# Zero products in TensorE's waits, halved fp32 casts, and batch 1 masked by VectorE in a fused attention and FFN kernel

## The chip, the cores and the metric

The kernel runs on one core of one Trainium2 chip. A core has five engines which run their own instruction queues in order: TensorE (PE in the profile; its weight loads are PEld), VectorE (DVE), ScalarE (ACT), GpSimd (POOL) and SyncE (SP). They wait for one another by semaphores. Transfers are issued from the queues of POOL, SP and ACT. The metric is the device time of one execution in microseconds; the median of five runs is compared.

## The reference

Attention with 8 heads over 8 batches of 576 positions of 64, followed by a multiplicative FFN.

```python
scores = scale * np.matmul(q, k.transpose(0, 1, 3, 2))
rel = pos[:, None] - pos[None, :]
mask_plain = (rel >= 0) & (rel < 32)
mask_dil = (rel >= 0) & (rel < 128) & (rel % 4 == 0)
# heads 0-3 take mask_plain, heads 4-7 mask_dil; softmax over the masked scores
x = attn_out, as 4608 tokens of 512
out = ((x @ w1) * (x @ w2)) @ w3 @ w_out
```

w1 and w2 are 512 x 1024, w3 is 1024 x 1024, w_out 1024 x 512. All tensors are float32 in memory. The kernel multiplies in bf16.

## The kernel before

Attention is done in blocks of 96 queries against 128 keys. A batch has two head halves u (0 plain, 1 dilated) of six blocks each. The FFN is done in units of 288 tokens, two to a batch.

The kernel writes out every piece of work as a task with an engine, an estimated duration and a priority, and a planner (class Plan) lays the tasks out in time and gives each a PSUM bank. The order that results is the program order of each engine's queue. The planner's times have no other part in the run: at run time an engine simply waits, in its queue, for the semaphores of what it needs. The tables RANK, ON_DVE and FIRST_LOADS set priorities, which evacuations VectorE does instead of ScalarE, and the order of the weight loads.

The names of the tasks, with batch b, half u and step i (two steps in each u):

- T: VectorE turns q, k and v into columns (`turn`, in 32 x 32 squares); C casts the first q and k from float32 on ScalarE (`round_rows`). Only these two transfers, the u = 0 half of q and k of batch 0, come in float32 through SP; every other load is converted on the way by POOL's transfers. POOL's transfers have eight semaphores in turn, so the ninth waits in the queue until the first has landed.
- S: the scores of a group of blocks on TensorE (`Group.scores`), in four PSUM banks; E: their exponential on ScalarE (`exps`). The task is named after its first block: S0.3 is the last of the four groups of batch 0. Batches below BIASED have groups of three blocks, in which four products of the identity with a 288-column bias first put the mask into PSUM (L400). The others have groups of GRP = 5, which run on across batches, and VectorE multiplies the exponentials by a 0/1 mask, half a group at a time (M, L436). The masks are made by GpSimd out of the bias.
- VT and VK: for batches 0 and 1 v is transposed on TensorE (`v_back`) and written back by ScalarE, or by VectorE for names in ON_DVE (`v_keep`).
- V: probabilities times v for one step (`Step.values`); R and N: reciprocal and normalization on VectorE; X: back transpose on TensorE for batches 0 and 1, K: its copy to XT (`keep`). Later batches use a transposing transfer on SP.
- W3T, W3C, W3M, W3D: per block of 128 rows of w3, transpose on TensorE (eight products of 128 columns), copy to w3T on ScalarE, product with w_out (eight of 512 columns), copy to wf_sb. So w3 and w_out are merged into one matrix inside the kernel.
- A, B: up-projections of a unit by w1 and w2, four products of 288 columns each (L525), with CA (copy on ScalarE) and G (product on VectorE); Y: down-projection, eight products of 512 columns (L552).

The first A needs the copies K0.0, K0.1 and K0.2. The first two units are done for the lower half of the w1, w2 columns and then for the upper. Each S is tied to a certain A, so that it doesn't run too early (LEAD).

Of the kernel before, what the change touches and what calls it, by code (L numbers as in the profile page):

```python
# [10 lines left out]
P = 128  # L11
# [17 lines left out]
BIG = 30000.0  # L29
BIASED = 2  # L30
TURNED = 2
DIRECT_V = 2
ORDER = (2, 3, 0, 1)
RES = (0, 2, 1, 3)
RANK = dict(E=3, VK=1, K=1.5, N=0.4, T=0.4, VT=0.4, S=0.3, V=0.05, X=0.4)
WARM = 12
FIRST_LOADS = ("30", "w0", "w1", "w2", "q1", "31", "k1", "o0", "o1", "32", "33", "34", "v1", "35", "36", "37")
SHIFT = {}
ON_DVE = ("K0.0", "K0.1", "K0.2", "K1.1", "K1.2", "K1.3", "VK1.1.0", "W3D3", "W3D4", "W3D7")
GRP = 5  # L40
WHOLE = ("qn", "kn")
BUSY = 4500
LEAD = 1.2

# [12 lines left out]
class Plan:  # L57
# [6 lines left out]
    def __init__(self):  # L64
        self.tasks, self.now, self.dma = [], None, 0.0

    def add(self, name, eng, dur, deps, fn, prio, slot=0, lat=150, after=()):
# [3 lines left out]

    def run(self):
        users = {id(t): [] for t in self.tasks}
        takers = {id(t): [] for t in self.tasks}
# [39 lines left out]
        while len(order) < n:  # L114
            progress = True
            while progress:
                progress = False
                for e in engines:
                    if free[e] > now:
                        continue  # L120
                    for r, t in sorted(waiting[e], key=lambda x: x[1].prio):
                        if r > now:
                            continue
                        at = place(t) if t.slot else 0
                        if at is not None:
                            break
                    else:
                        continue
                    waiting[e].remove((r, t))
                    t.start = now  # L130
                    if e == "DMA":
                        free[e] = now + t.dur[0]
                        if t.dur[1]:
                            dma = max(dma, now + t.dur[0]) + t.dur[1]
                            t.end = dma + 1900
                        else:
                            t.end = free[e]
                    else:
                        t.end = free[e] = now + t.dur
                        if e == "SP" and t.name[0] == "X" and dma > now:  # L140
                            t.end = free[e] = now + t.dur + BUSY
                            dma += 1.5 * t.dur
                    if t.slot:
                        t.place = at
                        held[at : at + t.slot] = [t] * t.slot
                        if t.slot == 4:
                            kept = None
                    order.append(t)
                    for u in users[id(t)]:
                        left[id(u)] -= 1  # L150
                        if not left[id(u)]:
                            r = max(d.end + (0 if d.eng == u.eng else d.lat) for d in u.deps)
                            waiting[u.eng].append((r, u))
                    progress = True
# [6 lines left out]
            now = min(ahead)  # L161
        return sorted(order, key=lambda t: t.start), now


@with_exitstack
def kernel(
# [74 lines left out]

    def round_rows(nm, u):
        at = {"qn": 0, "kn": 18 * D, "vn": 36 * D}[nm]
        if (nm, 0) not in qk:
            qk[(nm, 0)] = qk_pool.tile([P, 2, 18 * D], BF16, tag=nm, name=nm)
        nc.scalar.copy(out=qk[(nm, 0)][:, u, :], in_=stage[:, at : at + 18 * D])  # L246

# [95 lines left out]
    def turn(b, u, nm, part):  # L343


        src = qk[(nm, b)][:, u, :].bitcast(U32)
        dst, pad = {"qn": (qts, 0), "kn": (kts, PADK), "vn": (vts, PADK)}[nm]
        d = dst[b % len(dst)].rearrange("p u w c -> p u (w c)").bitcast(U32)[:, u, :]
        if part is None:
            o = d[:, pad : pad + S].rearrange("p (j a) -> p a j", a=18)  # L350
            nc.vector.transpose(out=o, in_=src.rearrange("p (a i) -> p a i", a=18))  # L351
            return
# [270 lines left out]
    add = plan.add  # L623

    def warm_up():
        o = bank(512)
# [7 lines left out]
    def constants():  # L634
# [5 lines left out]
        for t in vps:  # L640
            nc.vector.memset(t[:, :, :, D : D + 1], 1.0)
            nc.vector.memset(t[0:32, :, 0, 0:D], 0.0)

    c1 = add("const", "DVE", 1200, [], first_constants, -99)
    c0 = add("const2", "DVE", 1400, [c1], constants, -98)
    add("warm", "PE", 1840 + 216 * WARM, [c1], warm_up, 0)

# [37 lines left out]
    for i, nm in enumerate(WHOLE):  # L685
        t = add(f"LF{nm}", "SP", 100, [], lambda nm=nm: load_whole(nm, rows_of[nm], 0), -9 + i,
                lat=4400 + 1350 * i)
        L[(nm, 0, 0)] = add(f"C{nm}", "ACT", 1120, [t], lambda nm=nm: round_rows(nm, 0), -9 + i,
                            lat=100)
    plan.dma = 1200 + 1350 * len(WHOLE)  # L690
# [24 lines left out]
    for ft in sorted(lw3):  # L715
        x = add(f"W3T{ft}", "PE", 510, [lw3[ft], idt], lambda f=ft: w3_back(f), 6, slot=1,
                after=w3m[-3:-2])
        y = add("W3C", "ACT", 1012, [x], lambda f=ft: w3_keep(f), -1, lat=100, after=w3m[-3:-2])
        if ft + 7 in lw3:
# [12 lines left out]
    def turns(b, u, nm, pr):  # L732

        if u == 0:
            parts = (None,) if nm != "qn" else (0, 1)
        else:
            parts = (2, 3, 4, 5) if b == 0 else (0, 1)
        old = last_v.get((b - 1, u)) if nm == "vn" else last_s.get((b - 2, u))
        cost = {None: 1245, 0: 750, 1: 630, 2: 430, 3: 370, 4: 430, 5: 370}
        ts = [  # L740
            add(f"T{nm}{b}.{u}.{part or 0}", "DVE", cost[part], [L[(nm, b, u)], c0],
                lambda part=part: turn(b, u, nm, part), pr + (1 if part in (4, 5) else 0), lat=80,
# [5 lines left out]

    vals, T = {}, {}
    for b in range(B):  # L750
# [4 lines left out]
        for u in range(2):  # L755
            tk = turns(b, u, "kn", 10 * b + RANK["T"])
            tq = turns(b, u, "qn", 10 * b + RANK["T"])
            for hf in range(2):
                T[(b, u, hf)] = tk[hf] + tq[hf]
        for u in range(2):  # L760
            if b >= DIRECT_V:
                break
            tv = turns(b, u, "vn", 10 * b + RANK["T"])
            for half in range(2):
                x = add(f"VT{b}.{u}.{half}", "PE", 420, tv[half] + [idt],
                        lambda b=b, u=u, h=half: v_back(b, u, h), b - 99 + RANK["VT"], slot=1)
                last_v[(b, u)] = x
                name = f"VK{b}.{u}.{half}"
                eng, dur = ("DVE", 980) if name in ON_DVE else ("ACT", 880)
                vals[(b, u, half)] = [  # L770
                    add(name, eng, dur, [x, c0], lambda b=b, u=u, h=half, e=eng: v_keep(b, u, h, e),
                        10 * b + RANK["VK"], lat=100)
                ]
# [8 lines left out]
        def group(blocks, biased):  # L782
# [6 lines left out]
            if biased:  # L789
                s = add("S" + n, "PE", 980, need + [blk, idt], lambda: g.scores(True),  # L790
                        b - 99 + RANK["S"], slot=4)
                e = add("E" + n, "ACT", 1150, [s], g.exps, 10 * b + RANK["E"], lat=100, after=old)
                ms = [e]
            else:
                s = add("S" + n, "PE", 240 + 85 * g.n, need, g.scores, b - 99 + RANK["S"],
                        slot=4)
                e = add("E" + n, "ACT", 160 + 330 * g.n, [s], g.exps, 10 * b + RANK["E"], lat=100,
                        after=old)
# [4 lines left out]
                ]  # L803
            paced.append((b, 2 * u + m // 3, s))
            for i, x in enumerate(blocks):
                grp_of[x] = (n_grp, g, i, ms)
# [14 lines left out]
        while steps < 4 * B:  # L821
# [3 lines left out]
            if any(x not in grp_of for x in mine):  # L825
# [5 lines left out]
            ms = {id(t): t for x in mine for t in grp_of[x][3]}  # L831
            vv = add(f"V{n}", "PE", 420, list(ms.values()) + vals[(bb, u, hf)], st.values,
                     bb - 99 + RANK["V"], slot=2)
            for x in mine:
                readers.setdefault(grp_of[x][0], []).append(vv)
            rc = add(f"R{n}", "DVE", 240, [vv], st.recip, 10 * bb + RANK["N"], lat=0,
                     after=[prev["x"][i]])
            ns = [
                add(f"N{n}", "DVE", 960 if u == 0 else 555, [vv, rc],
                    lambda st=st, part=part: st.norm(part), 10 * bb + RANK["N"], lat=80)  # L840
                for part in ((None,) if u == 0 else (0, 1))
            ]
            if bb < TURNED:
                x = add("X" + n, "PE", 350, ns + [idt], st.back, bb - 99 + RANK["X"], slot=1)
                name = f"K{n}"
                eng, dur = ("DVE", 460) if name in ON_DVE else ("ACT", 640)
                x = add(name, eng, dur, [x], lambda st=st, eng=eng: st.keep(eng),
                        10 * bb + RANK["K"], lat=100)
            else:
# [54 lines left out]
    for b, i, t in paced:  # L904
        pair = int(16 * (b - LEAD) + 4 * i)
        if pair > 0:
            t.after.append(pairs[pair])
            t.deps.append(pairs[pair])

    order, _ = plan.run()  # L910
    for t in order:
# [32 lines left out]
```

## Time and profile before

| | |
|---|---|
| median of 5 runs | 256.76 us (256.68 to 256.77) |
| profiled execution | 256.81 us, its span 255.0 us |
| PE busy | 243.9 us, 96% of the span |
| DVE busy | 164.7 us, 65% |
| ACT busy | 123.9 us, 49% |
| POOL busy | 67.0 us, 26% |
| chain that ended last | PE 90%, of it L525 50%, L552 24% |
| up-projections L525 | 1024 products, first at 19.00 us |

The page has one row for each engine in 40 slices of 6.4 us, whose digits are tenths of busy time, and a row PEclk for the clock that the throttle granted to TensorE. In the timeline a line is a run of like instructions: start, length from the first start to the last end, engine, line, operation, result and operands, shapes, count. Brackets give idle time just before, and what ended it. Matmuls are pipelined: the length of a run holds the drain of its last product, and the next run can start before it.

### The profile page before, as it was taken

What the parts mean: (1) busy time and instruction counts of PE and PEld (TensorE: products, weight loads), DVE (VectorE), ACT (ScalarE), POOL (GpSimd) and SP (SyncE); (2) the same over time, 40 slices, a digit from 0 to 9 for tenths busy, and PEclk for the clock granted to TensorE, in tenths of its full rate; (3) what the DMA queues carried; (4) which work ended last, traced back from release to release, by engine and by line L of the source; (5) the groups of instructions that cost most, each with busy time, mean ns of one, the idle gap of its engine ahead of it and who ended that gap; (6) DMA issues with size and microseconds to landing.
All of it is one profiled execution on the core that took longest, in us unless ns stands there. A gap on an engine that the chain in (4) does not pass through costs nothing.

```text
span 255.0 us, 6714 instructions
## 1 busy us (share of the span) xinstructions
PE 243.9 (96%) x2700; PEld 167.5 (66%) x2732; DVE 164.7 (65%) x341; ACT 123.9 (49%) x216; POOL 67.0 (26%) x103
## 2 busy tenths in 40 slices
PE   7779999999999999999999999999999999999993
PEld 2468866765676666667676766676766766777661
DVE  3995773299889998888388684875746554333220
ACT  5774466763635355353553624554545534333331
POOL 7642219656403623631043040210000000000000
PEclk9999999999999999999999999999999999999999
DMA  7999999999997999999963939263141231711113
GB/s 226 204 200 210 209 208 212 206 96 185 145 191 166 205 174 187 173 189 186 181 94 56 100 59 143 85 89 87 44 87 45 66 90 55 94 41 41 44 41 123
DMA packets 59230, 33.40 MB, mean 131 GB/s; under 512 B 44736, under 2 KB 49088, under 8 KB 59200
## 3 DMA queue, kind: packets, MB, share of 16 engines
q0 software_dynamic: 38544, 18.81, 58.6%
q1 hardware_dynamic: 20512, 14.03, 25.1%
q8 instruction: 21, 0.34, 0.6%
q10 hardware_dynamic: 144, 0.13, 0.2%
q14 instruction: 9, 0.07, 0.1%
HBM read 38.80 MB, written 9.44 MB: 189 GB/s over the span
## 4 chain that ended last, share of the span: by engine, by line
PE 90%; DVE 5%; DMA 2%; ACT 1%; issue 1%; ACTq 0%; DVEq 0%
PE ps L525 50%; PE ps L552 24%; PE ps L606 5%; PE ps L453 4%; PE ps L417 3%; DMA gt<-in_q_dram 2%; PE ps L594 1%; DVE xo L476 1%; DVE qt L366 1%; ACT et L428 1%; PE ps L493 1%; PE ps L375 1%; DVE kt L366 0%; ACT qn L246 0%; DVE kt L351 0%
## 5 line engine op out<-in xcount | busy, mean ns | idle before, releaser
L525 PE MATMUL ps<-XT,w_sb 128*128 128x288 bf16 x1024 | 136.2, 286 | 0.5 <-DVE XT L503 0.3
L525 PEld LDWEIGHTS <-w_sb 128*128 128x128 bf16 x1024 | 97.9, 98 | 31.4 <-issue 0.5
L541 DVE TENSOR_TENSOR gt<-ps,asb 128x288 bf16<-128x288 f32 x128 | 58.0, 456 | 56.9 <-PE ps L525 55.4
L536 ACT CAST asb<-ps 128x288 bf16<-128x288 f32 x128 | 51.0, 399 | 63.3 <-PE ps L525 61.6
L552 PE MATMUL ps<-wf_sb,gt 128*128 128x512 bf16 x260 | 65.4, 379 | 1.4
L552 PEld LDWEIGHTS <-gt 128*128 128x128 bf16 x288 | 28.1, 98 | 27.6
L268 POOL DMA_DIRECT2D vp<-in_v_dram x48 | 30.5, 640 | 52.3 <-PE ps L453 31.4
L563 ACT COPY osb<-ps 128x512 f32<-128x512 f32 x35 | 20.5, 586 | 47.2 <-PE ps L552 45.4
L428 ACT ACTIVATE et<-ps 128x1920 bf16<-128x1920 f32 (+2 forms) x23 | 34.4, 1509 | 4.4 <-PE ps L417 2.8
L476 DVE TENSOR_TENSOR xo<-ps,rcp 96x384 bf16<-96x384 f32 (+1 forms) x48 | 31.6, 678 | 0.7
L366 DVE STREAM_TRANSPOSE qt<-qn 128x320 uint32<-128x320 uint32 (+3 forms) x34 | 22.5, 670 | 2.0 <-ACT qn L246 1.7
L436 DVE TENSOR_TENSOR et<-et,mask 128x960 bf16<-128x960 bf16 (+1 forms) x30 | 17.9, 631 | 6.0 <-ACT et L428 5.8
L453 PE MATMUL ps<-vp,et 128*128 128x65 bf16 x384 | 15.4, 193 | 0.5 <-ACT et L428 0.5
L453 PEld LDWEIGHTS <-et 128*128 128x128 bf16 x384 | 14.4, 98 | 1.8 <-issue 0.6
L606 PE MATMUL ps<-wo_sb,w3T 128*128 128x512 bf16 x60 | 14.6, 379 | 0.2
L417 PEld LDWEIGHTS <-kt 32*128 32x128 bf16 x768 | 9.2, 92 | 7.2 <-issue 4.9
L417 PE MATMUL ps<-qt,kt 32*128 32x96 bf16 x768 | 12.5, 201 | 1.5 <-DVE kt L351 1.5
L366 DVE STREAM_TRANSPOSE kt<-kn 128x320 uint32<-128x320 uint32 (+3 forms) x18 | 11.5, 639 | 1.9 <-PE ps L417 1.7
L254 POOL DMA_DIRECT2D vp<-in_v_dram x6 | 7.3, 1212 | 13.6 <-PE ps L453 13.6
L351 DVE STREAM_TRANSPOSE kt<-kn 128x576 uint32<-128x576 uint32 x8 | 10.0, 1248 | 0.8 <-PE ps L417 0.8
L606 PEld LDWEIGHTS <-w3T 128*128 128x128 bf16 x64 | 6.0, 97 | 6.2
L464 DVE RECIPROCAL rcp<-ps 96x12 f32<-96x12 f32 x32 | 6.9, 218 | 4.8 <-PE ps L453 4.5
(52 smaller groups left out, 107.4 us busy)
## 6 DMA issues: line engine op xcount, KB each, us to landing
qn<-in_q_dram POOLq DMA_DIRECT2D x7, 576.0 KB, 10.9
kn<-in_k_dram POOLq DMA_DIRECT2D x7, 576.0 KB, 8.6
w3n<-in_moe_w_dram POOLq DMA_DIRECT2D x8, 256.0 KB, 15.0
out_dram<-osb SPq DMA_DIRECT2D x7, 256.0 KB, 2.3
out_dram<-osb SPq DMA_DIRECT2D x8, 224.0 KB, 3.5
vp<-in_v_dram POOLq DMA_DIRECT2D x6, 288.0 KB, 10.5
out_dram<-osb SPq DMA_DIRECT2D x8, 192.0 KB, 2.7
out_dram<-osb SPq DMA_DIRECT2D x8, 160.0 KB, 2.7
```

Of the source, the lines that this page charges most:

```text
L268: nc.gpsimd.dma_start(out=vp[32 + p0 : 32 + p0 + n, 4:8, m, 0:D], in_=v_rows(b, 4, 4 * t0 + res, [[4 * D, n], [S * D, 4], [1, D]]),)
L366: nc.vector.transpose(out=o, in_=i)
L417: nc.tensor.matmul(out=self.sp[:, g, QB * i : QB * i + QB], lhsT=kt[prt, u, QB * m : QB * m + P, c], rhs=qq, start=(c == 0 and not biased) ...
L428: nc.scalar.activation(out=ev, in_=self.sp[:, :, 0:x], func=ACT.Exp, scale=scale)
L453: nc.tensor.matmul(out=self.o[:, g, mm, :], lhsT=grp.et[:, c0 : c0 + P], rhs=vps[self.b % 2][:, 4 * self.u + g, 3 * self.hf + mm, 0 : D + ...
L476: nc.vector.tensor_tensor(out=dst, in0=self.o[0:QB, hs, :, 0:D], in1=self.rcp[0:QB, hs, :].unsqueeze(3).to_broadcast([QB, n, 3, D]), op=AL ...
L525: nc.tensor.matmul(out=o, lhsT=w_sb[:, c, f * P : (f + 1) * P], rhs=unit_cols(k, c), start=(j == 0), stop=(j == DCH - 1),)
L536: nc.scalar.copy(out=a_sb, in_=held[("a", k, f)])
L541: nc.vector.tensor_tensor(out=gt[:, f, c0 : c0 + UNIT].rearrange("p (r m t) -> p m r t", r=2, m=BLK), in0=held[("b", k, f)].rearrange("p ( ...
L552: nc.tensor.matmul(out=y, lhsT=gt[:, f, c0 : c0 + P], rhs=wf_sb[:, f, :], start=(f == 0), stop=(f == KFF - 1),)
L563: nc.scalar.copy(out=o_sb, in_=held[("y", i)])
L606: nc.tensor.matmul(out=o, lhsT=w3T[ft][:, g, :], rhs=wo_sb[:, g, :], start=(g == 0), stop=(g == KFF - 1),)
```

## The change

- BIASED goes from 2 to 1: batch 1 is masked by VectorE, in the running groups of five blocks.
- While the planner finds TensorE idle, from its 2.0 us until the first A, it places a task `fill`: one product of zeros, 128 x 128 by 128 x 256, into a bank which nobody reads. The built program has 37 of them: 1 before the first scores, 4 before the third group's bias, 15 before S0.3, 15 before V0.3 and 2 before the first A. WARM goes from 12 to 14 products of 512 columns.
- The casts of the first q and k are made in two halves, and the turn of k in two (parts 6 and 7), each named as depending on its half.
- FIRST_LOADS: w3 blocks 0 and 1 before w1 and w2, block 2 between their middle and last columns; q and k of batch 1 behind w_out.
- RANK changes, and a table FIRST applies to batch 0. ON_DVE changes: VectorE gets VK0.0.1 and VK1.0.1, and gives up the six copies K and VK1.1.0; of the w3 copies it has blocks 1, 3 and 7 in place of 3, 4 and 7. LEAD goes from 1.2 to 1.1.
- Some of the planner's durations change. LATE is off and does nothing.

In the built program S0.3 moves behind V0.1, V0.2, X0.0 and X0.1 on TensorE, and two W3T in place of one stand before the first A. From the fifth unit on the mix of pieces is the same, in a slightly different order.

```diff
-BIASED = 2
+BIASED = 1
+LATE = False
...
-RANK = dict(E=3, VK=1, K=1.5, N=0.4, T=0.4, VT=0.4, S=0.3, V=0.05, X=0.4)
-WARM = 12
-FIRST_LOADS = ("30", "w0", "w1", "w2", "q1", "31", "k1", "o0", "o1", "32", "33", "34", "v1", "35", "36", "37")
+RANK = dict(E=0.4, VK=2, K=0.3, N=1.5, T=3, VT=0.3, S=0.4, V=0.05, X=0.2, W=6, C=-1)
+FIRST = {"E": 2, "VK": 0.4, "K": 0.5, "N": 0.2, "T": 2, "VT": 0.05, "S": 0.2, "V": 0.05, "X": 0.4}
+WARM = 14
+FILL = 110
+FIRST_LOADS = ("30", "31", "w0", "w1", "32", "w2", "o0", "o1", "q1", "k1", "33", "34", "v1", "35", "36", "37")
 SHIFT = {}
-ON_DVE = ("K0.0", "K0.1", "K0.2", "K1.1", "K1.2", "K1.3", "VK1.1.0", "W3D3", "W3D4", "W3D7")
+ON_DVE = ("VK0.0.1", "VK1.0.1", "W3D1", "W3D3", "W3D7")
...
-LEAD = 1.2
+LEAD = 1.1
...
                     else:
+                        idle = e == "PE" and now >= self.fill_from and self.fill_to.start is None
+                        f = Task("fill", "PE", FILL, [], self.fill, 0, 1, 0, ())
+                        at = place(f) if idle else None
+                        if at is None:
+                            continue
+                        f.start, f.end, f.place = now, now + f.dur, at
+                        free[e], held[at] = f.end, f
+                        users[id(f)], takers[id(f)] = [], []
+                        fills.append(f)
                         continue
...
-        return sorted(order, key=lambda t: t.start), now
+        return sorted(order + fills, key=lambda t: t.start), now
...
-    def round_rows(nm, u):
+    def round_rows(nm, u, half):
...
-        nc.scalar.copy(out=qk[(nm, 0)][:, u, :], in_=stage[:, at : at + 18 * D])
+        o, i = qk[(nm, 0)][:, u, :], stage[:, at : at + 18 * D]
+        if nm == "qn":
+            n, c0 = ((5, 0), (4, 2 * D))[half]
+            o, i = (
+                bass.AP(tensor=x.tensor, offset=x.offset + c0, ap=[x.ap[0], [4 * D, n], [1, 2 * D]])
+                for x in (o, i)
+            )
+        else:
+            c = slice(9 * D * half, 9 * D * half + 9 * D)
+            o, i = o[:, c], i[:, c]
+        nc.scalar.copy(out=o, in_=i)
...
-        if part is None:
+        if part in (None, 6, 7):
+            a = slice(0, 18) if part is None else slice(9 * part - 54, 9 * part - 45)
             o = d[:, pad : pad + S].rearrange("p (j a) -> p a j", a=18)
-            nc.vector.transpose(out=o, in_=src.rearrange("p (a i) -> p a i", a=18))
+            i = src.rearrange("p (a i) -> p a i", a=18)
+            nc.vector.transpose(out=o[:, a, :], in_=i[:, a, :])
             return
...
+    def rank(kind, b):
+        return (RANK if b else FIRST)[kind]
...
+    def fill():
+        nc.tensor.matmul(out=bank(256), lhsT=warm[:, 0:P], rhs=warm[:, 0:256], start=True, stop=True)
+
+    plan.fill, plan.fill_from = fill, 2000
...
+    plan.fill_to = pairs[0]
     order, _ = plan.run()
```

## The prediction

> **What bounds the kernel now.** I read the page first: busy time, the slices, and the chain that ended last.
>
> ```profile
> span 255.0 us, 6714 instructions
> ...
> PE 243.9 (96%) x2700; PEld 167.5 (66%) x2732; DVE 164.7 (65%) x341; ACT 123.9 (49%) x216; POOL 67.0 (26%) x103
> ...
> PE   7779999999999999999999999999999999999993
> ...
> PEclk9999999999999999999999999999999999999999
> ...
> PE 90%; DVE 5%; DMA 2%; ACT 1%; issue 1%; ACTq 0%; DVEq 0%
> ```
>
> TensorE (PE) is the bound. Only its first three slices (to about 19 us) are not full. So the time is a sum: when PE reaches the first up-projection (L525), plus PE work left from there, plus its later waits. I check the sum on this execution. From the first up-projection on there are 1024 products of 288 columns at 122.5 ns start to start (80 in 9.8 us on the chain), 36 down-projections and 8 w3 products of 1.73 us (eight times 216 ns), and about 29 us of smaller pieces: 231 us. Added to 19.0 this is 250.0; the last product ends at 250.8, and 4.2 us of evacuation and store follow. The waits after 19 us are thus together under 1 us. The execution took 256.81 us, 1.8 around the span; the median is 256.76, so a change of the span carries over one for one.
>
> Next the timeline at the two places which the change touches. Columns: start, length, engine, line.
>
> ```profile
> 15.05 0.65 PE L400 MATMUL ps<-bias,ident 128*128 128x288 bf16 x4
> 15.64 0.44 PE L417 MATMUL ps<-qt,kt 32*128 32x96 bf16 x24
> 16.16 1.14 ACT L428 ACTIVATE et<-ps 128x1152 bf16<-128x1152 f32 x1
> 17.18 0.81 ACT L385 COPY vp<-ps 128x768 bf16<-128x768 bf16 x1
> 17.94 1.00 DVE L503 COPY XT<-ps 128x576 bf16<-128x576 bf16 x2
> 19.00 1.63 PE L525 MATMUL ps<-XT,w_sb 128*128 128x288 bf16 x12 [0.25 <-DVE XT L503]
> ```
>
> The fourth score group of batch 0 (S0.3) starts at 15.05, and 3.95 us later the first up-projection runs. VectorE (DVE) does the last copies to XT while ScalarE (ACT) does the exponential and the values.
>
> ```profile
> 34.89 0.65 PE L400 MATMUL ps<-bias,ident 128*128 128x288 bf16 x4
> 37.15 0.65 PE L400 MATMUL ps<-bias,ident 128*128 128x288 bf16 x4 [0.27 <-ACT et L428]
> 38.76 0.44 PE L417 MATMUL ps<-qt,kt 32*128 32x96 bf16 x24
> 39.41 0.65 PE L525 MATMUL ps<-XT,w_sb 128*128 128x288 bf16 x4 [0.22 <-ACT et L428]
> ...
> 61.93 0.62 PE L417 MATMUL ps<-qt,kt 32*128 32x96 bf16 x40
> 62.48 0.67 PE L525 MATMUL ps<-XT,w_sb 128*128 128x288 bf16 x4
> ```
>
> Batch 1's four biased groups hold PE from 34.89 to 39.41: 4.52 us for 12 blocks, waits for ACT included. An unbiased group of five takes 0.55, plus 0.10 to switch to it (the 12 products before it start at 60.36, and 1.47 later would be 61.83): 0.65 us.
>
> **The change, part by part.**
>
> *Batch 1 without bias.* Four biased groups go. In all there are then 84 unbiased blocks, 16 groups of five and one of four, against 14 and one of two: two fives (1.30) and 16 small products more (40 take about 0.42, so 0.17). PE: -4.52 + 1.47 = **-3.05 us**. ACT pays 2.4 exponentials of 1.77 for four of 1.13, about equal. DVE gets some five mask products of 0.65, 3.1 us in all; three copies of 0.45 leave it in exchange. GpSimd's masks keep their place behind the same loads and should end near 44 as now, before the first mask product is due near 46.
>
> *One more w3 transpose early.* Blocks 0 and 1 now both transpose before the first up-projection. One times eight products at 56 ns: **-0.45 us**. Their two ACT copies (1.02 each) also come early, between VK0.1.0 and the copies to XT.
>
> *fp32 halves.* A cast of 1152 elements takes 1.15. With bf16 copies of 96 elements at 0.27 the line is 0.19 us plus 0.84 ns an element: halves of q 0.72 and 0.62, of k 0.67 each. That starts the first transpose early only if it waits for its own half. In the built program the first q transpose waits for the count which the second q cast sets. Both q casts end at about 6.16 instead of 6.07. K's halves do help: its cast and transpose overlap, but DVE is by then the limit. A half of kt is not in the trace; forms of 256 and 320 elements take 0.65 and 0.76, so 0.70, bounds 0.65 and 0.76. [...] The trace has 1.25 for the whole and its successor starting 1.09 after it, so an operation's last 0.16 lies under the next; by that row two halves take 1.08 start to start, as long as the whole. [...]
>
> *The start of the up-projections.* This is the large loss. DVE runs without a gap in both kernels until N0.1, the second normalization: from 6.2, two q parts 1.3, k 1.1, v 1.1, four q parts 1.5 and two k parts 0.75 (0.50 and 0.25 in turn), VK0.0.1, now on DVE, 0.90, two v parts 0.75, and twice reciprocal plus normalization 1.15-1.2: 15.9 (16.1 now). Then X0.1 on PE, to 16.2. Behind it PE's queue has **15 zero products, and only then S0.3** (now S0.3 stands before V0.2 and X0.1). Its last kt parts also moved, on DVE, behind N0.1 (ready 16.7), and its four banks wait for N0.2, whose end I put at about 17.85. A zero product of 256 columns is not in the trace; between 128 columns (56 ns) and 288 (122.5) it is 109. 15 are 1.64: S0.3 starts at 17.86, **2.8 us later than now**. From there: bias products and scores 0.9, exponential seen by ACT at 18.94, to 20.07; VK0.1.1 to 20.8; K0.2, now on ACT and queued behind both, to 21.3. PE meanwhile has 15 zero products from 19.4 to 21.05, V0.3 0.37 and two more 0.22: first up-projection at 21.6, **+2.6 us**. Bounds +2.2 (no zero product is in the way) and +3.1 (each at 125 ns).
>
> *What the zero products buy.* The row to weigh is PE's first wait: between its bias products and first scores it idles 1.46 us, and the stretches below keep the granted clock at 1.00.
>
> ```profile
> 8.00:10.00 2.00, 1.23 (x52) 0.87 (x52) 2.00 (x3) 0.74 (x1) 1.25 (x2) 1.00 1.10 205
> 16.00:18.00 2.00, 1.50 (x35) 1.22 (x27) 1.71 (x6) 1.99 (x3) 0.85 (x2) 1.00 1.43 198
> ```
>
> (length; busy of PE, PEld, DVE, ACT, POOL; clock; DMA share; GB/s.) No row shows a wait of 1.7, which the new order would have without them. [...] The two more warm products end by 7.5, before the scores can start: nothing.
>
> *The order of loads.* w3 block 1 (256 KB written, 1.3 us at 205 GB/s) now precedes w1 and w2. From the lanes' issue waits the first pair lands near 16 now, so near 17.3; PE comes at 21.6. The last halves land near 24 now, so near 26.5; they are needed eight pairs of 0.98 and some smaller pieces after 21.6, near 30. q and k of batch 1 go behind w_out; both sets have the same bytes, and k lands near 38 instead of 31. The scores of batch 1 come near 43. All hidden, by 4 us or more for the weights.
>
> *The w3 stretch.* With ACT's queue as written, w3 copies stand behind exponentials of 1.77. Block 3's transpose ends at 43.8 and its copy at 44.9, which PE needs at 44.7; block 4's copy starts behind E1.0 at 46.4, ends at 47.5, needed at 47.2; a third one likewise. Together **+0.8**, bounds 0 and 1.6.
>
> *Sum.* +2.6 - 3.05 - 0.45 + 0.8 = -0.1. Small waits of before (some 0.1) may go: -0.2. 256.76 - 0.2 = **256.6 us**.
>
> **The rivals.** (1) *Near tie*, as summed: bias work is exchanged for the late start. Own range 256.25 to 257.3. Chance 0.45. (2) *The w3 waits don't appear* and the start is a little earlier: for it, that w3 work can stand in for a late group; against it, the order of ACT's queue. -0.8 and -0.2 from the sum: **255.6**. Chance 0.33. (3) *Slower: VectorE becomes the bound between 40 and 57 us.* W3D1 stands in its queue before the second q transpose of batch 1 and waits for the second w3 product (39.5). From 39.7 on come W3D1 and W3D3 (1.3), q and k transposes (4.5), two gates (0.9), four mask products (2.4), v transposes (2.5), VK1.0.1 (0.9) and three reciprocals with normalizations (3.6): 55.8, and about 57 with the waits for batch 1's k and for V. PE then needs X1.2 and K1.2 (0.3 and 0.65 with their lags and a copy ahead in ACT's queue: 59.1) for a unit which could start near 59.3. For it: DVE is 93% busy from 50 to 60 now. Against it: from 40 to 50 only 36%. If that line is two mask products longer (1.3), PE waits 1.05: **257.6**. It ends slower once the line is 0.9 longer. Chance 0.22.
>
> **How the numbers follow.** 0.2% of 256.76 is 0.5 us, about what a measurement tells from no change. The tie case lies mostly within it: of its 0.45, 0.03 falls on the faster and 0.02 on the slower side, and the neighbours give 0.03 and 0.04 back. Faster 0.33, same 0.47, slower 0.20. The range takes in both rivals and the start's bounds: 255.5 to 257.6.
>
> **What would show it.** S0.3's bias products (L428) near 17.9 and the first L553 near 21.6; 37 products of L676; L553 at 41 to 43 followed by L445 x40 in place of L428; PE's waits for w3T near 45 and 47.5; from 60 us on the same pieces as before. Wrong if L553 starts before 20.5 or after 22.5, or if PE's waits for VectorE between 45 and 60 pass 1 us.

## The result and the profile after

| | before | changed |
|---|---|---|
| median | 256.79 us (75 runs) | 256.37 us (40 runs) |
| profiled execution | 256.81 us, span 255.0 | 256.57 us, span 254.8 |
| first up-projection | 19.00 | 21.54 |
| third unit starts | 60.36 | 59.13 |

The ratio is 0.9979, with a 95% interval of 0.9972 to 0.9985: faster by 0.21%, 0.42 us, at the edge of what a measurement of this kernel can tell. One thing is needed to read the numbers below: in some executions of before and of two of the variants the mean clock granted to TensorE is about 0.99 in place of 1.00 (in the two that were traced it is at half for one stretch of 3.41 us early on), and these take about 0.7 to 1.1 us longer.

The page after, in its rows for the engines, the clock and the chain that ended last:

```profile
span 254.8 us, 6758 instructions
...
PE 245.1 (96%) x2723; PEld 169.4 (66%) x2755; DVE 165.3 (65%) x341; ACT 126.0 (49%) x221; POOL 66.1 (26%) x103
...
PE   7799999999999999999999999999999999999993
...
PEclk9999999999999999999999999999999999999999
...
PE 88%; DMA 5%; ACT 3%; DVE 2%; issue 1%; ACTq 0%; DVEq 0%
```

PE is as full as before. Its busy time has grown by 1.2 us although bias products have gone, since 37 zero products have come. New on the chain are 3% of ScalarE and more of transfers (5% in place of 2%).

The start of the up-projections, PE in the timeline of after:

```profile
16.11 1.80 PE L676 MATMUL ps<-warm 128*128 128x256 bf16 x15
17.75 0.65 PE L428 MATMUL ps<-bias,ident 128*128 128x288 bf16 x4
18.34 0.44 PE L445 MATMUL ps<-qt,kt 32*128 32x96 bf16 x24
...
19.06 0.42 PE L521 MATMUL ps<-ident,xo 96*128 96x96 bf16 x6
19.32 1.80 PE L676 MATMUL ps<-warm 128*128 128x256 bf16 x15
20.95 0.53 PE L481 MATMUL ps<-vp,et 128*128 128x65 bf16 x12
...
21.54 1.63 PE L553 MATMUL ps<-XT,w_sb 128*128 128x288 bf16 x12
```

PE looks busy without a break from 16 to 21.5 us, yet the two groups of 15 products in it (L676) are zeros. The fourth score group (L428, L445) starts at 17.75 where before had it at 15.05. ScalarE in the same stretch tells what the first up-projection waits for (L529 copies to XT, L456 is the exponential, L413 the copy VK0.1.1):

```profile
16.87 1.22 ACT L529 COPY XT<-ps 128x576 bf16<-128x576 bf16 x2
18.83 1.13 ACT L456 ACTIVATE et<-ps 128x1152 bf16<-128x1152 f32 x1 [0.74 <-PE ps L445]
19.85 0.79 ACT L413 COPY vp<-ps 128x768 bf16<-128x768 bf16 x1
20.53 0.66 ACT L529 COPY XT<-ps 128x576 bf16<-128x576 bf16 x1
```

Two of the three copies to XT that it needs end by 18.1. The third, K0.2, runs at 20.53 behind the exponential and VK0.1.1, because its transpose X0.2 stands on PE behind the fourth score group (19.06 above).

Batch 1 and the w3 products, PE in the timeline of after:

```profile
43.65 0.62 PE L445 MATMUL ps<-qt,kt 32*128 32x96 bf16 x40
44.20 0.62 PE L622 MATMUL ps<-ident,w3n 128*128 128x128 bf16 x8
44.82 1.90 PE L634 MATMUL ps<-wo_sb,w3T 128*128 128x512 bf16 x7
46.65 0.61 PE L445 MATMUL ps<-qt,kt 32*128 32x96 bf16 x40
47.40 1.90 PE L634 MATMUL ps<-wo_sb,w3T 128*128 128x512 bf16 x7
...
50.27 0.61 PE L622 MATMUL ps<-ident,w3n 128*128 128x128 bf16 x8
50.89 1.90 PE L634 MATMUL ps<-wo_sb,w3T 128*128 128x512 bf16 x8
...
57.41 1.89 PE L634 MATMUL ps<-wo_sb,w3T 128*128 128x512 bf16 x8
59.13 0.65 PE L553 MATMUL ps<-XT,w_sb 128*128 128x288 bf16 x4
```

Two groups of five blocks (L445) take the place of four biased ones; L622 transposes a block of w3 and L634 is its product with w_out. Three small gaps stand ahead of w3 products. After the transpose at 44.20 eight products at 56 ns would end the issue at 44.65, and L634 starts at 44.82: 0.17. After the scores at 46.65, issued by 47.20, it starts at 47.40: 0.20. After 50.27 it is 0.17 again: together 0.54 us. ScalarE, where the copies to w3T (L629) stand among the exponentials:

```profile
43.75 1.01 ACT L629 COPY w3T<-ps 128x1024 bf16<-128x1024 bf16 x1 [0.49 <-PE ps L622]
44.66 1.78 ACT L456 ACTIVATE et<-ps 128x1920 bf16<-128x1920 f32 x1
46.32 1.02 ACT L629 COPY w3T<-ps 128x1024 bf16<-128x1024 bf16 x1
47.31 1.77 ACT L456 ACTIVATE et<-ps 128x1920 bf16<-128x1920 f32 x1
...
57.58 1.19 ACT L529 COPY XT<-ps 128x576 bf16<-128x576 bf16 x2
```

The copies end at 44.76 and 47.34, and the w3 products start 0.06 after each. The last line holds the copies to XT that the third unit needs.

### The profile page after: what moved, and what is told of

Same layout as the page of the kernel before. It is cut to its first block, busy times and chain, and to the rows that moved or that the text cites. A ratio compares the mean times of both kernels' runs of the same rounds, so it can differ in the third digit from the quotient of the medians.

```text
span 254.8 us, 6758 instructions
## 1 busy us (share of the span) xinstructions
PE 245.1 (96%) x2723; PEld 169.4 (66%) x2755; DVE 165.3 (65%) x341; ACT 126.0 (49%) x221; POOL 66.1 (26%) x103
## 3 DMA queue, kind: packets, MB, share of 16 engines
q0 software_dynamic: 38544, 18.81, 57.7%
## 4 chain that ended last, share of the span: by engine, by line
PE 88%; DMA 5%; ACT 3%; DVE 2%; issue 1%; ACTq 0%; DVEq 0%
PE ps L553 49%; PE ps L580 22%; PE ps L634 5%; PE ps L481 4%; PE ps L445 3%; DMA XT<-xo 3%; DMA gt<-in_q_dram 2%; ACT et L456 2%; PE ps L676 2%; PE ps L622 1%; PE ps L403 1%; PE ps L521 1%; ACT w3T L629 1%; DVE qt L394 1%; ACT qn L271 0%
## 5 line engine op out<-in xcount | busy, mean ns | idle before, releaser
L569 DVE TENSOR_TENSOR gt<-ps,asb 128x288 bf16<-128x288 f32 x128 | 57.7, 455 | 52.1 <-PE ps L553 49.8
L293 POOL DMA_DIRECT2D vp<-in_v_dram x48 | 29.7, 625 | 42.3 <-PE ps L481 18.5
L456 ACT ACTIVATE et<-ps 128x1920 bf16<-128x1920 f32 (+2 forms) x21 | 34.2, 1633 | 5.5 <-PE ps L445 4.8
L504 DVE TENSOR_TENSOR xo<-ps,rcp 96x384 bf16<-96x384 f32 (+1 forms) x48 | 31.5, 676 | 0.6
L464 DVE TENSOR_TENSOR et<-et,mask 128x960 bf16<-128x960 bf16 (+1 forms) x34 | 21.4, 646 | 4.8 <-ACT et L456 4.7
L634 PE MATMUL ps<-wo_sb,w3T 128*128 128x512 bf16 x60 | 14.4, 379 | 0.4
L445 PE MATMUL ps<-qt,kt 32*128 32x96 bf16 x768 | 12.1, 201 | 1.4 <-DVE kt L379 1.4
L445 PEld LDWEIGHTS <-kt 32*128 32x128 bf16 x768 | 9.1, 92 | 6.5 <-issue 4.5
L245 POOL DMA_DIRECT2D kn<-in_k_dram x8 | 5.5, 686 | 27.3 <-DVE kt L394 14.9
L379 DVE STREAM_TRANSPOSE kt<-kn 128x576 uint32<-128x576 uint32 (+1 forms) x9 | 9.9, 1123 | 1.4 <-PE ps L445 1.4
L634 PEld LDWEIGHTS <-w3T 128*128 128x128 bf16 x64 | 5.9, 98 | 6.8 <-ACT w3T L629 0.6
```

The lines of the kernel that those rows point to most:

```text
L293: nc.gpsimd.dma_start(out=vp[32 + p0 : 32 + p0 + n, 4:8, m, 0:D], in_=v_rows(b, 4, 4 * t0 + res, [[4 * D, n], [S * D, 4], [1, D]]),)
L445: nc.tensor.matmul(out=self.sp[:, g, QB * i : QB * i + QB], lhsT=kt[prt, u, QB * m : QB * m + P, c], rhs=qq, start=(c == 0 and not biased) ...
L456: nc.scalar.activation(out=ev, in_=self.sp[:, :, 0:x], func=ACT.Exp, scale=scale)
L464: nc.vector.tensor_tensor(out=ev, in0=ev, in1=mk, op=AL.mult)
L504: nc.vector.tensor_tensor(out=dst, in0=self.o[0:QB, hs, :, 0:D], in1=self.rcp[0:QB, hs, :].unsqueeze(3).to_broadcast([QB, n, 3, D]), op=AL ...
L569: nc.vector.tensor_tensor(out=gt[:, f, c0 : c0 + UNIT].rearrange("p (r m t) -> p m r t", r=2, m=BLK), in0=held[("b", k, f)].rearrange("p ( ...
```

## The experiments

All kernels here compute the whole result. The kernel before, in the runs made beside these, had a median of 256.86 us (23 runs, 256.71 to 258.14).

### The order of the changed kernel without its zero products

```diff
     def fill():
-        nc.tensor.matmul(out=bank(256), lhsT=warm[:, 0:P], rhs=warm[:, 0:256], start=True, stop=True)
+        return
```

The planner still places the zero products and lays all other work around them, but no instruction is issued for them. Only they are left out.

> The changed kernel's order of every queue is kept, but the 37 zero products are left out of TensorE's queue (two more warm products stay). Theory (the zero products stand in the way of late work, and the order that was planned around them costs more): first up-projection at 21.0 instead of 21.5, time 0.5 to 0.6 us below the changed kernel, 255.8; granted clock 1.00 in every stretch although TensorE then waits about 1.7 us twice. Rival (they keep the clock up): the clock falls to a half before the first up-projections, those take 240 ns each for some microseconds, and the time rises by 1 to 2 us.

Measured: 256.92 us (255.9 to 258.54, 12 runs), ratio to before 0.9987, 0.9967 to 1.0007. PE in the timeline of this variant:

```profile
17.55 0.28 PE L428 MATMUL ps<-bias,ident 128*128 128x288 bf16 x1 [0.75 <-DVE xo L504]
18.02 0.28 PE L428 MATMUL ps<-bias,ident 128*128 128x288 bf16 x1 [0.18 <-DVE xo L504]
18.24 0.44 PE L445 MATMUL ps<-qt,kt 32*128 32x96 bf16 x24
...
20.60 0.82 PE L481 MATMUL ps<-vp,et 128*128 128x65 bf16 x12 [1.00 <-ACT vp L413]
21.23 2.92 PE L553 MATMUL ps<-XT,w_sb 128*128 128x288 bf16 x12
```

Two things are read here. First, the place that the zero products had is now a wait: for the banks which the second normalization of N0.2 (L504) holds until 17.97, and then for the values copied by ScalarE. The scores start at 18.24 in place of 18.34 and the first up-projection at 21.23 in place of 21.54. So in this order the zero products themselves cost only some 0.3 us of the late start; the order costs the rest. In this execution ScalarE can cast the first q only 0.28 us later, since its transfer ends later, and the first scores start at 9.08 in place of 8.80; counted from there the zero products cost 0.59. Second, the last line: twelve up-projections take 2.92 us, where after needs 1.63. Here are two stretches of 3.41 us of the same variant (length; busy of PE, PEld, DVE, ACT, POOL; granted clock; DMA share; GB/s):

```profile
17.02:20.44 3.42, 1.70 (x38) 1.10 (x38) 1.73 (x4) 3.00 (x6) 1.41 (x3) 1.00 1.33 201
20.44:23.85 3.41, 3.25 (x23) 2.27 (x23) 1.66 (x4) 1.05 (x3) 1.10 (x2) 0.50 1.24 207
```

PE is busy for half of the first, with no single wait in it over 1.0 us, and the clock is 0.50 for the whole of the second. The rival was right for such executions. In the 12 there are five whose mean granted clock is 0.993 or less, with 256.82, 257.01, 257.31, 257.68 and 258.54 us. The other seven have 255.9 to 257.39; their median is 256.61, so that even at full clock nothing is gained on the 256.37 of the changed kernel. Only the fastest meets the 255.8 of the theory, and why two at a mean clock of 0.998 and 1.000 take 257.39 and 257.14 is open.

### The changed kernel planned without zero products

```diff
-                        idle = e == "PE" and now >= self.fill_from and self.fill_to.start is None
+                        idle = False
```

Here they are neither issued nor planned, so other work moves into their place.

> The planner of the changed kernel places no zero products and orders the rest anew (the banks which they took are free for it); all else as in the changed kernel. Theory (the late start comes from the zero products through the plan's banks, not from ON_DVE or FIRST): the first up-projection moves to 19.2, the time to 1.0 us below the changed kernel, 255.4. Rival of the prediction (the late start comes from the copies K and VK0.1.1 on ScalarE, behind the last exponential, and from VectorE's line; at best 0.4 us of it is due to the zero products): first up-projection at 21.0 to 21.5, time 255.9 or more.

Measured: 255.26 us (255.1 to 256.21, 6 runs), ratio 0.9924, 0.9900 to 0.9947. By the medians it is faster than both kernels, by 1.1 us than the changed one. The numbers of the theory came (18.83 and 255.26), those of the rival did not. PE in its timeline:

```profile
16.92 0.30 PE L521 MATMUL ps<-ident,xo 96*128 96x96 bf16 x3 [0.80 <-DVE xo L504]
...
17.52 0.66 PE L428 MATMUL ps<-bias,ident 128*128 128x288 bf16 x4
18.11 0.44 PE L445 MATMUL ps<-qt,kt 32*128 32x96 bf16 x24
...
18.83 2.61 PE L553 MATMUL ps<-XT,w_sb 128*128 128x288 bf16 x20
...
24.87 10.94 PE L553 MATMUL ps<-XT,w_sb 128*128 128x288 bf16 x88 [0.89 <-ACT XT L529]
...
57.77 0.65 PE L553 MATMUL ps<-XT,w_sb 128*128 128x288 bf16 x4
```

And ScalarE of the same variant:

```profile
16.72 1.76 ACT L529 COPY XT<-ps 128x576 bf16<-128x576 bf16 x3
18.60 1.13 ACT L456 ACTIVATE et<-ps 128x1152 bf16<-128x1152 f32 x1
```

The fourth score group is only 0.23 us earlier than in the changed kernel (17.52). What moved is X0.2, which now stands ahead of it. All three copies to XT are done in one piece at 18.5, ahead of the exponential in place of behind it, and the up-projections start 2.71 us earlier, at 18.83. Of that, 0.89 is given back at 24.0 to 24.9, where PE waits for the next copy to XT (L529). Another 0.37 is only moved: V0.3, twelve products, now comes after the first up-projections, at 21.28 in place of 20.95. That leaves 1.45; the third unit starts 1.36 earlier, and the medians differ by 1.11. The theory put the late start down to the plan's banks; whether a bank or the time that the zero products take moved X0.2 in the plan, no run separates.

### Only batch 1's masks on the kernel before

```diff
-BIASED = 2
+BIASED = 1
```

> The kernel before with BIASED = 1 and nothing else. Theory (the gain of the change is batch 1's bias products, 2.3 to 3.0 us less on TensorE, minus new waits in the w3 stretch and one group more after it): first up-projection unchanged at 19.0, the third unit near 57.7 instead of 60.4, time 1.0 us below the kernel before, 255.8. Rival (VectorE's masks make it the bound between 40 and 57 us): the third unit not before 59.5, time 256.8 or more.

Measured: 256.73 us (255.74 to 257.4, 12 runs), ratio 0.9971, 0.9953 to 0.9990. In the profiled execution, of 256.95 us, the clock falls here too, in another place (one line of PE's timeline, then stretches with the columns as above):

```profile
8.94 0.67 PE L417 MATMUL ps<-qt,kt 32*128 32x96 bf16 x24 [2.30 <-DVE kt L351]
...
5.31:8.72 3.41, 1.33 (x8) 0.59 (x6) 2.40 (x3) 2.09 (x2) 3.11 (x5) 1.00 1.11 213
8.72:12.14 3.42, 3.20 (x61) 2.27 (x62) 3.35 (x10) 1.94 (x2) 1.61 (x3) 0.50 1.10 204
```

PE is busy for 39% of the first stretch. The longest wait in it is 2.30 us, from the bias products at 5.99 to the scores at 8.94, which wait for DVE's kt. The first up-projection comes at 20.04, 1.04 us later than in before, and the third unit at 58.73. Without the 1.04 that would be the 57.7 of the theory, and the rival's 59.5 is not reached. Six of the 12 executions have a mean clock of 0.992 or 0.993 and 256.72 to 257.4 us. Of the six at 0.996 and above, five lie between 255.74 and 256.25, which is the theory's 255.8 and up to 0.4 more, and one at 257.01, which stays open.

The mask alone thus gains about 0.8 us on the kernel before, not 3: the ratio makes 0.74, and among executions at full clock the medians are 255.98 of six and 256.79 of 14. Two waits behind the third unit, in the timeline, are part of what is missing:

```profile
61.80 0.62 PE L417 MATMUL ps<-qt,kt 32*128 32x96 bf16 x40 [0.30 <-ACT et L428]
...
83.01 0.59 PE L417 MATMUL ps<-qt,kt 32*128 32x96 bf16 x37 [0.39 <-ACT asb L536]
```

With the waits of 0.62 and 0.28 for DVE among the scores at 37.9 and 38.4 they make 1.6 us of new waits, which before's tables do not hide. Of the way from 3.05 to 0.8 that leaves some 0.6 us unaccounted for, and how far an execution at full clock has the same waits no trace here shows.

### The changed kernel with batch 1's bias back

```diff
-BIASED = 1
+BIASED = 2
```

> The changed kernel with BIASED = 2 (batch 1 gets its bias products again). Theory: the late start at 21.5 stays and the gain is gone: third unit near 63.5, time 2.5 to 3.0 us above the changed kernel, 259. Rival (the masks by VectorE bring less than 1 us here): below 257.4.

Measured: 259.45 us (259.27 to 259.61, 6 runs), ratio 1.0080, 1.0059 to 1.0101. PE in its timeline:

```profile
21.61 1.63 PE L553 MATMUL ps<-XT,w_sb 128*128 128x288 bf16 x12
...
63.70 2.12 PE L553 MATMUL ps<-XT,w_sb 128*128 128x288 bf16 x16
```

The start is that of the changed kernel (21.61), the third unit starts at 63.70, and the time is 3.08 us longer. The theory was right and the rival wrong. So the masks are worth 3.08 us in the changed kernel's tables. Against the two medians of before, the rest of the change makes it 2.6 to 2.7 us slower, and the masks pay that back with little over.

## Why the prediction was right, and where its steps were not

The forecast was 256.6 us, and 256.37 came, inside the likeliest case's own range of 256.25 to 257.3. Its sum, term by term:

| term | predicted | measured | from |
|---|---|---|---|
| start of the up-projections | +2.6 | +2.54 | 19.00 and 21.54 |
| batch 1 without bias | -3.05 | -3.08, with the waits for w3T in it | bias put back, whole kernel |
| one more w3 transpose early | -0.45 | not measured apart | |
| waits for w3T | +0.8 | +0.54 | three gaps above |
| sum | -0.1 | -1.0 with the -0.45 as forecast | +2.54 - 3.08 - 0.45 |
| small waits of before that go | -0.1 | not measured apart | |
| result | -0.2 | -0.42 | medians |

The large terms, the late start against the bias products, were right, and so was their near tie. That the number came so close is in part luck. Masks and waits for w3T together were forecast at -2.25 and brought -3.08: the variant with the bias back has no such gap ahead of its w3 products, so the 0.54 is in the 3.08 already. Against that stand 0.5 to 0.6 us of costs which no term of the forecast has. They show in that variant too: it is 2.66 us slower than before, where its start and the early transpose make +2.61 - 0.45 = 2.16. What they are is open.

*The start.* The steps on its way came as worked out: S0.3's bias at 17.75 (17.86 forecast), its exponential at 18.83 (18.94), K0.2 at 20.53 (20.8), the first up-projection at 21.54 (21.6). The lower bound, +2.2 when no zero product is in the way, is nearly met: 21.23 against 19.00 in the order without them, of which 0.28 is its late first scores. But it held for that order alone. In an order planned without them the start is at 18.83, and the whole loss is gone. The prediction put the loss down to the fourth group's place behind the zero products and the second normalization; the run planned without them shows the group just as late (17.52) and the start early. What sets it, by the two timelines, is that X0.2, and so K0.2, comes behind the group and its exponential; no run moved X0.2 alone. The prediction had K0.2 in its queue "behind both" and did not ask what its being there cost: 2.7 us at the start, the zero products with it.

*The waits for w3T* were mis-sized: 0.54 for 0.8. The copies end at 44.76 and 47.34, forecast 44.9 and 47.5. The mechanism, a copy behind an exponential, is the one foreseen.

*The zero products.* This step failed: the sum counts nothing for them, as if before had no loss of clock to save. The row weighed for it has a wait of 1.46 us at full clock; what a wait of 1.7 us does to the clock no row of before showed. The runs show the clock falling after stretches in which PE was busy 50% and 39%, whose longest waits were 1.00 and 2.30 us. And before does have such a loss. Of its 23 executions beside the experiments nine have a mean clock of 0.990 to 0.992 and take 257.56 to 258.14 us; the other 14, at 0.996 and above, take 256.71 to 257.11. The profiled execution of before was at full clock, and by their times the five given with it (256.68 to 256.77) were too. Of the 75 executions in the table of the result 23 take 257.54 us or more and the others at most 257.17; their clock is not on record. None of the 40 executions of the changed kernel is under 0.996. The median hides that gain, since in both kernels it falls among the executions at full clock: the medians differ by 0.42, the means (257.05 and 256.50) by 0.55. Where the clock falls in before no trace shows; the variant of before with masks, which runs the same first products, has its fall at 8.72, after a stretch which the two more warm products make fuller (an estimate: at 216 ns each they bring it from 1.33 to 1.76 of 3.41 us, 52%). How the gain divides between the warm and the zero products was not run apart. Leaving the zero products out of the changed order brings the fall back, in 5 of 12 executions. But the variant planned without them keeps the 14 warm products, and none of its six executions is under 0.997: there the zero products may not be needed, though six are too few to tell.

*VectorE as the bound* didn't come, but was near. The copies to XT (L529) before the third unit end on ScalarE at 58.77, and the unit starts at 59.13, when PE is through its w3 products: 0.36 us to spare, where the prediction put the turning point at 0.9.

*Halves and loads.* In the trace the halves gain nothing. The two q casts run from 4.93 to 6.17, the first q transpose starts at 6.21 (6.10 in before), and the first scores at 8.80 (8.77). On VectorE the two halves of k take 1.24 us (7.51 to 8.75), but the next transpose starts at 8.59, 1.08 after the start of the first half; before had 1.09 for the whole. So the row's value was right: the halves last 0.70 us each, but the second starts 0.54 after the first, and from start to start the two take no longer here than the whole. The order of loads cost no wait on PE that the trace shows. Neither was run as a change of its own, so both are read from the trace of after alone.

*From 60 us on* the pieces are not quite the same as before. In program order 16 score products (0.22 us), 12 value products (0.37) and six transposes (0.25) that before does ahead of the third unit stand behind it now: 0.84. So the third unit is 1.23 earlier and the end 0.42. One more thing was not foreseen. The chain of after (start, length, what) holds a transposing transfer:

```profile
84.05 8.47 DMA XT<-xo
92.56 5.06 PE ps L553 x40
```

PE starts the up-projections of that unit when it has landed, some 0.2 us after its last value product was issued (24 products from 91.62, 0.73). It took 8.47 us here, against a median of 4.6 in this trace. Before's chain holds none, although its slowest transfer of this kind took 9.5. Of the 40 executions 14 lie above 256.5, up to 257.33, at mean clocks of 0.997 and above. That such a landing makes them is likely, but no run tested it.

## What to carry to other kernels

A filler that a planner places like work also takes a bank and a place in the order; here the 37 products themselves cost 0.3 to 0.6 us of the start, and together with the order planned around them 1.1 us of the whole time. After an order has moved, ask of every queue which short copy on the path now stands behind a long instruction; it was K0.2 behind an exponential, not the exponential itself. And look at the granted clock of several executions before a loss of clock is put at nothing: the profiled run of before had 1.00, and 9 of 23 others of the same kernel had 0.990 to 0.992.

## What the runs showed of the hardware

In the two falls recorded here while PE had work, the longest idle gap ahead was 1.00 us in the one and 2.30 in the other. Both last one stretch of 3.41 us, and each follows a stretch of the same length in which PE was busy for 50% or 39% of the time. In these traces such stretches form a grid: the pieces of the clock record at 1.00 are 3.413 and 242.346 us long in the masked variant, 13.653 and 232.106 in the changed order without zero products, and 249.173 in the other four, which is 1 and 71, 4 and 68, and 73 times 3.413. The grid does not start with the kernel. In the six traces the record begins between 4.64 and 7.37 us, at 5.31 in the masked variant and at 6.67 in before, although both run the same first products. Up to that point the warm products follow one another every 427 ns and behind it every 216, so the clock is at half until then; the 1.00 that PEclk prints for that time is not a record.

In before the stretch from that boundary holds more work, and so does a stretch at its end, in which PE has its last products (columns as above):

```profile
6.67:10.09 3.42, 1.96 (x57) 1.19 (x55) 3.38 (x5) 1.58 (x2) 2.58 (x4) 1.00 1.09 203
10.09:13.50 3.41, 2.90 (x68) 2.20 (x59) 3.27 (x12) 3.41 (x5) 1.60 (x4) 1.00 1.23 200
...
249.02:252.43 3.41, 1.76 (x9) 0.59 (x6) 0.42 (x1) 0.96 (x2) 0.00 (x0) 1.00 0.52 162
252.43:255.84 3.41, 0.00 (x0) 0.00 (x0) 0.00 (x0) 0.00 (x0) 0.00 (x0) 1.00 0.15 50
```

PE is busy for 57% of the first and 52% of the third, and the clock stays at 1.00 in the next; only behind the empty last one, at 255.84 in the clock record, does it fall. In the variant planned without zero products a wait of 1.96 us, longer than any in the first of the two falls, costs nothing, since the boundary at 8.05 cuts it:

```profile
4.64:8.05 3.41, 2.10 (x12) 0.89 (x10) 1.91 (x4) 2.49 (x4) 3.20 (x6) 1.00 1.09 235
8.05:11.46 3.41, 2.31 (x65) 1.78 (x66) 3.34 (x8) 2.27 (x3) 1.78 (x3) 1.00 1.12 210
```

So what counts in these traces is the busy share of a whole stretch, and whether one and the same wait costs the clock depends on where the boundary falls. In all six, every stretch from the first boundary on with 52% or more is followed by one at full clock, and those with 50% or less by a fall. In these traces the limit thus lies between 50 and 52% of the profile's busy time, in which the ends of the products are modelled. That the place of the boundary is what parts the executions of before into 256.8 us and 257.6 and more is likely, but none of its slower ones was traced.
